# Seven block products for eight in the w_out matmul of an mLSTM-and-MLP kernel

## The chip, the cores and the metric

The kernel runs on one core of a Trainium2 chip. The metric is the device time of one execution in microseconds; smaller is better. Engines are named as in the profile: PE is TensorE (PEld its weight loads), DVE is VectorE, ACT is ScalarE, POOL is GpSimd, SP is SyncE.

## The reference

An mLSTM cell for batch 4, 8 heads, 768 steps and head dimension 40; its output (3072 tokens of 320 features) goes through an MLP with 2048 hidden features and the activation h - tanh(h). All is fp32, with weights that arrive as float64.

```python
for t in range(S):
    m_new = np.maximum(f_gate[:, :, t] + m, i_gate[:, :, t])
    f_stab = np.exp(f_gate[:, :, t] + m - m_new)
    i_stab = np.exp(i_gate[:, :, t] - m_new)
    m = m_new
    C = f_stab[:, :, None, None] * C + i_stab[:, :, None, None] * np.einsum('bhd,bhe->bhde', vt, kt)
    n = f_stab[:, :, None] * n + i_stab[:, :, None] * kt
    h_tilde = np.einsum('bhde,bhe->bhd', C, qt)
    denom = np.maximum(np.abs(np.einsum('bhd,bhd->bh', n, qt)[:, :, None]), 1.0)
    y[:, :, t] = h_tilde / (1.0 + np.exp(-o_gate[:, :, t])) / denom
x = y.transpose(0, 2, 1, 3).reshape(B * S, H * D)      # 3072 x 320
h = x @ w_in                                           # 320 x 2048
return (h - np.tanh(h)) @ w_out                        # 2048 x 320
```

## The kernel before

**Units.** The cell is cut into 24 units: 128 steps of one batch entry, all heads; unit n is chunk n // 4 of batch entry n % 4. A unit's steps are: `scores` (the products `ps`, masked on DVE into `P`), `inter` and `intra` (products of the state and of `P` with the scaled values `vs`, both into the PSUM tile `ph`), `gate` (on DVE: three short `den` rows, then `o` and `ys`, the last of which reads `ph` too), `update` (products `pc`, from which DVE's two `state` rows make the next chunk's state), and `turn` (three transposes into `px`, which ACT copies into `xT`).

**Groups, pairs, items.** Two units make a group of 256 tokens; there are 12 groups. The 16 blocks of 128 hidden features make 8 pairs. A (group, pair) takes an `up` (`ph_up` = xT times w_in: per feature block two full products of 256 columns and one over 64 rows, `w_rest`), a `shrink` (ACT: `z`, `q`; DVE: four `gt` rows, giving g = h - tanh h as a polynomial), and a `down`: four products `po` of 128x128 by 128x320, two token tiles times two feature blocks. Two pairs make an item; pairs 0, 1 and 8 stand alone. There are 50 items. The list of pairs first runs through the first four groups as the cell and the weights come (`RUNS`; partial sums go to `part`), then takes groups 4 to 11 one after another (`FIRST` = 4), each accumulated over its 8 pairs in `po` and copied out once.

**Order.** PE's order is written out: in step x of the main loop, `up` of item x, then `down` of item x - 1 (`LAG` = 1), and between them, in proportion to cost, the small steps of cell and weight conversion that `spread_over` put at x. A cell slot (`cell_slot`, line 510) holds the scores of unit s, the inside of unit o = s - 1 and the turn of x = s - 2. The order on DVE and ACT is the scheduler's from the main loop on (`Pinned.on = False`).

**Weights.** Each block of w_in and w_out is fetched as float64 bits by POOL and turned to fp32 by DVE and ACT (`weights`, rows `w_e`, `w_m`, `w_r`, then `w_in`, `w_rest`, `w_out`), eight staging buffers deep, in the first 150 us or so.

**PSUM.** Eight banks: `ph0`, `ph1` for `up`, `po0`, `po1` for `down` (line 580), two for scores, and two for the small tiles of the cell (`ph`, `pc`, `px` and those of the gates), a pool with `bufs=2` and one tag, line 173, from which each tile takes a free buffer:

```python
ps_b = ctx.enter_context(tc.tile_pool(name="ps_b", bufs=2, space=PSUM))
...
t["px"] = ps_b.tile([128, NK + 1, L], FP, name="px", tag="b")
```

Helpers record PE's, DVE's and ACT's operations, so the profile puts most of them on lines 102, 126 and 130, and tiles tell them apart.

Of the kernel before, what the change touches and what calls it, by code (L numbers as in the profile page):

```python
# [40 lines left out]
FP = mybir.dt.float32  # L44
# [28 lines left out]
def kernel(  # L73
# [96 lines left out]
    ps_h = ctx.enter_context(tc.tile_pool(name="ps_h", bufs=1, space=PSUM))  # L170
    ps_o = ctx.enter_context(tc.tile_pool(name="ps_o", bufs=1, space=PSUM))
    ps_a = ctx.enter_context(tc.tile_pool(name="ps_a", bufs=1, space=PSUM))
    ps_b = ctx.enter_context(tc.tile_pool(name="ps_b", bufs=2, space=PSUM))

# [97 lines left out]
    def gates(c0, c1, idle):  # L272

        t0, t1, cs, n = c0 * L, c1 * L, slice(c0, c1), c1 - c0
        at = slice(t0, t1)
        V.tensor_tensor_scan(out=m_sb[:, at], data0=f_sb[:, at], data1=i_sb[:, at],
                             initial=m_sb[:, t0 - 1:t0] if t0 else -1.0e30, op0=OP.add, op1=OP.max)
        if t0 == 0:

            V.memset(lf[:, 0:1], 0.0)  # L280
            t0 = 1
        V.tensor_tensor(out=lf[:, t0:t1], in0=f_sb[:, t0:t1], in1=m_sb[:, t0 - 1:t1 - 1], op=OP.add)
        V.tensor_tensor(out=lf[:, t0:t1], in0=lf[:, t0:t1], in1=m_sb[:, t0:t1], op=OP.subtract)
        V.tensor_tensor(out=i_sb[:, at], in0=i_sb[:, at], in1=m_sb[:, at], op=OP.subtract)

        cols = []
        for row in (lf, i_sb):
            p = ps_b.tile([L, NT, BH], FP, name="pcol", tag="b")
            for c in range(c0, c1):
                T.transpose(p[:, c, :], row[:, c * L:(c + 1) * L], ident[0:BH, 0:BH])  # L290
            cols.append(p[:, cs])
        V.tensor_copy(out=lfT[:, cs], in_=cols[0])
        A.activation(out=ei[:, 2, cs], in_=cols[1], func=AF.Exp)
        awake(idle)

        def sums_of(w):
            p = ps_b.tile([w.shape[1], NT, BH], FP, name="psum_lf", tag="b")
# [162 lines left out]
    def inter(n, j):  # L460
        t = un[n]
        if "ph" not in t:
            t["ph"] = ps_b.tile([L, H, D1], FP, name="ph", tag="b")
# [21 lines left out]
    def update(n, j):  # L485
        t = un[n]
        st = state[t["b"]][(t["c"] + 1) % 2]
        if j == 0:
            t["pc"] = ps_b.tile([TOP, HH, 2, D1], FP, name="pc", tag="b")
        T.matmul(t["pc"][:, j].rearrange("p two d -> p (two d)"), pair(t["k"], j), pair(t["vs"][:, 1], j), start=True, stop=True)  # L490
        if j < HH - 1:
            return
        for i in range(2):
            new, pc = st[:, :, i, :], t["pc"][:, :, i, :]
            if t["c"]:
                V.scalar_tensor_tensor(out=new, in0=pc, scalar=own[0:TOP, i:i + 1], in1=new, op0=OP.mult, op1=OP.add)
            else:
                V.tensor_single_scalar(new, pc, own[0:TOP, i:i + 1], op=OP.mult)

    def turn(n, j):  # L500
        t = un[n]
        if j == 0:
            t["px"] = ps_b.tile([128, NK + 1, L], FP, name="px", tag="b")
        T.transpose(t["px"][:, j, :], t["y"][:, FROM[j]:FROM[j] + 128], ident)
        if j == NK:
            g, tt = divmod(n, GT)
            A.copy(out=xT[g % NX][:, :, tt * L:(tt + 1) * L], in_=t["px"])
            un.pop(n)

    def cell_slot(s, o, x):  # L510


        steps = []
        if o is not None:
            prepare(o)
        if s is not None and s - 1 in un:
            prepare(s - 1)
        if s is not None:
            if s + 1 < NU and s + 1 not in ld:
                load_unit(s + 1)  # L520
            begin(s)
        for d in range(HH):
# [7 lines left out]
        if x is not None:  # L530
            steps += [(0.11, lambda j=j: turn(x, j)) for j in range(NK + 1)]
        return steps


    gT, po = {}, {}

    def up(some, shrink):

# [18 lines left out]
    def shrink(x):  # L557
        def steps(some, ph):
# [9 lines left out]
                V.scalar_tensor_tensor(out=gt[i], in0=ph[i], scalar=TINY_POLY[0], in1=z[i], op0=OP.mult, op1=OP.mult)  # L568
            for i in range(2):
                V.scalar_tensor_tensor(out=gt[i], in0=q[i], scalar=TINY_POLY[2], in1=gt[i], op0=OP.add, op1=OP.mult)  # L570

        return steps

    def down(x, some, g, p, first, last):
# [9 lines left out]
        def evict(tt):  # L584
            n = g * GT + tt
            if last < NP - 1:
                if first:
                    V.tensor_tensor(out=part[n], in0=po[tt], in1=part[n], op=OP.add)
                else:
                    A.copy(out=part[n], in_=po[tt])  # L590
                return
            ob = mlp.tile([128, DM], FP, name="ob", tag="ob")
# [4 lines left out]
            c, b = divmod(n, B)  # L597
            r0 = (b * NT + c) * L
            nc.scalar.dma_start(out=out[r0:r0 + L, :], in_=ob)

        return [(0.54, lambda i=i, tt=tt: product(i, tt)) for tt in range(GT) for i in range(2)]

# [12 lines left out]

    slots = [tuple(n if 0 <= n < NU else None for n in (s, s - 1, s - 2)) for s in range(NU + 2)]
    AHEAD = 3
    slots[AHEAD] = (3, 2, None)  # L620
    NS = len(slots)
# [5 lines left out]
    for g in range(FIRST, NG):  # L627
        pairs += [(g, p, 0, NP - 1) for p in range(NP)]

    ALONE = (0, 1, 8)  # L630
    items = []
    while sum(map(len, items)) < len(pairs):
        x = sum(map(len, items))
# [2 lines left out]
    def item(x):  # L636

        return min(i for i in range(len(items)) if sum(map(len, items[:i + 1])) > x)
# [19 lines left out]
    for i, (x0, x1) in enumerate(spans):  # L658
        begins[int(x0)].append((slots[AHEAD + i], x0, x1))

    first, steps = convert()
# [3 lines left out]
        due[p] = max(min(due[p], due[p + 1] - 1.25), 0.5)  # L667
    for p in range(1, NP):
        spread_over(steps[ready[p - 1]:ready[p]], due[p - 1], due[p])

    for fetch, _, _ in first:
        fetch()
# [52 lines left out]
    for x in range(len(items) + LAG):  # L725
# [2 lines left out]
        dense = []  # L728
        new = []
        for slot, x0, x1 in begins[x]:  # L730
            spread_over(cell_slot(*slot), x0, x1)
            if slot[0] is not None:
                new.append(slot[0])
        if x < len(items):
# [3 lines left out]
        dense += [(0.9, lambda n=n: halves(scores(n))) for n in new[1 if x < len(items) else 0:]]  # L738
        if x >= LAG:
            some = tuple(run[:2] for run in items[x - LAG])  # L740
            for i, run in enumerate(items[x - LAG]):
                dense += down(i, some, *run)
        merge(dense, [(cost, step) for _, cost, step in sorted(work[x], key=lambda w: w[0])])


# [4 lines left out]
    def rows_of_f():  # L750
# [11 lines left out]
        V.scalar_tensor_tensor(out=f, in0=f, scalar=1.0, in1=n, op0=OP.add, op1=OP.mult)  # L762


        row = ps_b.tile([NR, 2, L], FP, name="row", tag="b")
# [59 lines left out]
    with tc.If(nc.values_load(again, min_val=0, max_val=128,  # L825
                              skip_runtime_bounds_check_because="it counts partitions") > 0):
        T.last = V.last = A.last = None
        G.tensor_copy(out=diag, in_=ident.unsqueeze(1).to_broadcast([128, H, L]))
        V.tensor_copy(out=ei[:, 0], in_=ei[:, 2])
        V.memset(inv, 1.0)  # L830
        rows_of_f()
        for g in range(NG):
# [25 lines left out]
                            T.matmul(ob[tt], gts[i][:, p - p0, tt * L:(tt + 1) * L], w_out[:, 2 * p + i, :],  # L858
                                     start=(p == 0 and i == 0), stop=(p == NP - 1 and i == 1))
            for tt in range(GT):  # L860
                o = mlp.tile([128, DM], FP, name="ob", tag="ob")
# [44 lines left out]
```

## Time and profile before

| | |
|---|---|
| runs, us | 619.99, 620.53, 626.17 (median 620.53) |
| profiled execution, its own time, us | 618.87 |
| its span, first to last instruction, us | 617.2 |
| mean granted TensorE clock | 0.977 |
| PE busy, us | 573.7 (93%) |
| PEld busy, us | 444.0 (72%) |
| DVE busy, us | 297.4 (48%) |
| ACT busy, us | 194.7 (32%) |
| `po` products | 768 passes, 248.8 us |
| `ph_up` products, w_in and w_rest | 768 and 384 passes, 204.0 and 55.0 us |

An fp32 product is two passes on PE, so 384 `po` products are 768 rows. Busy time counts overlapping passes once, and a row's mean includes the tail that overlaps the next; the pitch of passes is read from their starts. In the rows of 40 slices a digit is tenths of a slice of 15.4 us.

### The profile page before, as it was taken

Reading aid. Unit: us, or ns where it says so; the run is one execution under the profiler, and the core shown is the slowest. Engines: PE = TensorE matmul, PEld = TensorE weight load, DVE = VectorE, ACT = ScalarE, POOL = GpSimd, SP = SyncE. Lnnn points to the kernel's source line nnn. Section 1 sums busy time; section 2 is a strip of 40 time slices with the busy share of each in tenths; the row PEclk is TensorE's granted clock in tenths of the full one; section 3 lists DMA queues with packets and bytes.
Section 4 is the critical chain, followed back from the end, with each engine's and each line's share of the span. In section 5 each row is a group of like instructions: output and inputs, shape, how many; then the busy total and the mean of one; then the engine's idle time right before and its main releaser. Section 6 shows DMA issues by size and latency. Waiting matters only on the chain.

```text
span 617.2 us, 8489 instructions
## 1 busy us (share of the span) xinstructions
PE 573.7 (93%) x3137; PEld 444.0 (72%) x3137; DVE 297.4 (48%) x716; ACT 194.7 (32%) x490; POOL 28.5 (5%) x60
## 2 busy tenths in 40 slices
PE   4965899998999999899999999999999999999995
PEld 1855777777787776777777787777778777767773
DVE  1679799999627334552623425325152333232231
ACT  1345554456123123221313214123141322232231
POOL 2022111220000000000000000000000000000000
PEclk9976699999999999999999999999999999999999
DMA  7665354452102010131212212011000000000000
GB/s 196 210 203 154 98 158 135 142 166 60 44 21 65 15 50 23 44 95 55 57 29 65 64 33 65 22 33 44 12 11 12 1 21 1 1 22 2 21 1 27
DMA packets 40865, 38.19 MB, mean 62 GB/s; under 512 B 3856, under 2 KB 38352, under 8 KB 40816
## 3 DMA queue, kind: packets, MB, share of 16 engines
q1 hardware_dynamic: 33000, 22.82, 12.9%
q0 software_dynamic: 2800, 9.18, 5.1%
q10 hardware_dynamic: 5016, 5.57, 2.7%
q8 instruction: 27, 0.44, 0.3%
q14 instruction: 22, 0.18, 0.1%
HBM read 33.62 MB, written 3.93 MB: 61 GB/s over the span
## 4 chain that ended last, share of the span: by engine, by line
PE 52%; issue 6%; ACT 2%; DVE 1%; ACTq 0%; DVEq 0%
PE ph_up L126 24%; PE po L126 23%; PE ph L126 3%; PE ps L126 1%; ACT q L102 1%; ACT z L102 1%; PE px L130 1%; PE pc L126 1%; DVE P L102 0%; ACT ob L102 0%; DVE gt L102 0%; DVE ob L102 0%; DVE part L102 0%; ACTq L102 0%; DVEq L102 0%
## 5 line engine op out<-in xcount | busy, mean ns | idle before, releaser
L126 PE MATMUL po<-w_out,gt 128*128 128x320 f32 x768 | 248.8, 449 | 12.4 <-DVE part L102 8.8
L126 PE MATMUL ph_up<-xT,w_in 128*128 128x256 f32 x768 | 204.0, 394 | 3.5 <-ACT xT L102 3.5
L102 DVE SCALAR_TENSOR_TENSOR gt<-ph_up,z 128x512 f32<-128x512 f32 (+1 forms) x100 | 62.5, 664 | 239.3 <-ACT z L102 239.2
L126 PEld LDWEIGHTS po<-w_out,gt 128*128 128x128 f32 x768 | 130.7, 191 | 57.3 <-DVE part L102 11.9
L126 PEld LDWEIGHTS ph_up<-xT,w_in 128*128 128x128 f32 x768 | 136.6, 193 | 22.8 <-ACT xT L102 4.6
L102 ACT ACTIVATE z<-ph_up 128x512 f32<-128x512 f32 (+1 forms) x100 | 57.1, 576 | 265.8 <-issue 143.7
L126 PEld LDWEIGHTS ph<-vs,P 128*128 128x128 f32 x384 | 70.7, 205 | 24.9 <-issue 6.3
L126 PE MATMUL ph<-vs,P 128*128 128x41 f32 x384 | 64.0, 264 | 5.9 <-DVE vs L102 3.1
L102 ACT ACTIVATE q<-z,tiny 128x512 f32<-128x512 f32 (+1 forms) x100 | 64.7, 700 | 0.0
L102 DVE SCALAR_TENSOR_TENSOR gt<-q,gt 128x512 f32<-128x512 f32 (+1 forms) x100 | 62.3, 661 | 0.0
L126 PE MATMUL ph_up<-xT,w_rest 64*128 64x256 f32 x384 | 55.0, 403 | 0.0
L126 PEld LDWEIGHTS ph_up<-xT,w_rest 64*128 64x128 f32 x384 | 32.9, 186 | 15.5 <-issue 12.5
L126 PEld LDWEIGHTS ph<-state,q 80*128 80x128 f32 x160 | 29.8, 194 | 8.3 <-ACT xT L102 0.5
L102 DVE TENSOR_TENSOR P<-ps,upto 128x512 f32<-128x512 f32 x48 | 30.9, 681 | 2.3 <-PE ps L126 2.3
L126 PEld LDWEIGHTS pc<-vs,k 128*80 128x80 f32 x160 | 22.3, 162 | 11.2 <-issue 3.2
L126 PEld LDWEIGHTS ps<-qz,kz 40*128 40x128 f32 x384 | 28.0, 205 | 2.2 <-DVE P L102 0.8
L126 PE MATMUL ph<-state,q 80*128 80x82 f32 x160 | 29.0, 262 | 0.3
L126 PE MATMUL ps<-qz,kz 40*128 40x128 f32 x384 | 29.1, 293 | 0.0
L126 PE MATMUL pc<-vs,k 128*80 128x82 f32 x160 | 25.2, 255 | 1.2 <-issue 1.2
L102 ACT ACTIVATE w_e<-w_e,rebias 128x256 int32<-128x256 int32 (+2 forms) x40 | 19.9, 503 | 20.1 <-DVE w_e L102 19.9
L102 ACT ACTIVATE w_r<-w 128x256 f32<-128x256 uint32 (+2 forms) x40 | 17.3, 434 | 20.1 <-DVE w_in L102 9.8
L335 POOL DMA_DIRECT2D w<-in_moe_w_in x35 | 19.0, 547 | 47.4 <-issue 21.0
(75 smaller groups left out, 305.6 us busy)
## 6 DMA issues: line engine op xcount, KB each, us to landing
w<-in_moe_w_out POOLq DMA_DIRECT2D x14, 320.0 KB, 3.5
kz<-in_kT SPq DMA_DIRECT2D x48, 80.0 KB
v<-in_v SPq DMA_DIRECT2D x24, 160.0 KB
k<-in_k SPq DMA_DIRECT2D x24, 160.0 KB
o<-in_o_gate SPq DMA_DIRECT2D x24, 160.0 KB
out<-ob ACTq DMA_DIRECT2D x24, 160.0 KB
qz<-in_qT SPq DMA_DIRECT2D x44, 80.0 KB
q<-in_qT SPq DMA_DIRECT2D x40, 80.0 KB
```

The source lines that it names most:

```text
L102: i = method(*args, **kwargs)
L126: return cls.keep(nc.tensor.matmul(*args, **kwargs))
L130: return cls.keep(nc.tensor.transpose(*args, **kwargs))
L335: queue.dma_start(out=to[rows, cols], in_=part)
```

## The change

For groups 4 to 10 (`SEVEN`) the `down` of a pair is computed in the seven-product form: the two token tiles by two feature blocks of g, and the two feature blocks by two halves of 160 output columns of w_out, are taken as 2x2 blocks; seven block products of 128x128 by 128x160 take the place of eight (four products of 320 columns). For this DVE makes four sums of w_out's blocks per pair once (`sums_of_weights`, 128x160 each) and four sums of g per item (`sums_of_g`, 128x256 each). The seven results of a group are gathered in three PSUM banks, `pS0`, `pS1` and `pS2`, and `put_together` joins them at the group's end into the two output tiles.

The third bank, `pS2`, is b1, one of the cell's two. The small tiles now come from the helper `small`, which hands out the tags b0 and b1 in turn; from the first slot that ends after item 18 on, b1 is taken off its list. From there `cell_slot` runs in the form `single`: inside, gate, update and turn of one unit one after the other in the one bank, with empty steps (`pause`) between, and the turn in the same slot as the inside, so there is one slot less. Pair 31 becomes an item of its own, so that items 18 to 49 hold two pairs of one group each; the slots after item 7 span 2.47 items each instead of 2.25.

```diff
-    ps_b = ctx.enter_context(tc.tile_pool(name="ps_b", bufs=2, space=PSUM))
+    ps_b = ctx.enter_context(tc.tile_pool(name="ps_b", bufs=1, space=PSUM))
+    banks = ["b0", "b1"]
+    def small(shape, name):
+        banks.append(banks.pop(0))
+        return ps_b.tile(shape, FP, name=name, tag=banks[-1])
...
-            t["px"] = ps_b.tile([128, NK + 1, L], FP, name="px", tag="b")
+            t["px"] = small([128, NK + 1, L], "px")
...
+        if single:
+            steps += turning
+            if o is not None:
+                for d in range(HH):
+                    steps.append((0.22 if o >= B else 0.0, lambda d=d: inter(o, d)))
+                    steps += [(0.22, lambda h=h: intra(o, h)) for h in (2 * d, 2 * d + 1)]
+                steps.append((0.0, lambda: gate(o)))
+                un[o]["turned"] = True
+                pause = [(0.0, lambda: None)]
+                steps += 5 * pause
+                if o + B < NU:
+                    steps += [(0.18, lambda j=j: update(o, j)) for j in range(HH)] + 4 * pause
+                steps += [(0.11, lambda j=j: turn(o, j)) for j in range(NK + 1)] + 4 * pause
+            return steps
...
+    def sums_of_weights(p):
+        t = wT[p] = conv.tile([128, 4, HM], FP, name="wT", tag="w64", bufs=8)
+        even, odd = (w_out[:, 2 * p + i, :].rearrange("p (two n) -> p two n", two=2) for i in range(2))
+        return [... for o, a, b in (
+            (t[:, 0], even[:, 1], even[:, 0]), (t[:, 1], odd[:, 1], t[:, 0]),
+            (t[:, 2], odd[:, 1], even[:, 1]), (t[:, 3], odd[:, 0], t[:, 1]))]
+    def sums_of_g(some):
...
+        V.tensor_tensor(out=s3, in0=a[0][0], in1=a[1][0], op=OP.subtract)
+        V.tensor_tensor(out=s1, in0=a[1][0], in1=a[1][1], op=OP.add)
+        V.tensor_tensor(out=s2, in0=s1, in1=a[0][0], op=OP.subtract)
+        V.tensor_tensor(out=s4, in0=a[0][1], in1=s2, op=OP.subtract)
+    def down_seven(some):
...
+        for k in range(7):
+            for x, (_, p) in enumerate(some):
...
+                where, a, b = (
+                    ((0, 2), a11, even[:, 0]), ((0, 0), a12, odd[:, 0]), ((2, 1), a22, wT[p][:, 3]),
+                    ((1, 1), s3, wT[p][:, 2]), ((1, 0), s1, wT[p][:, 0]), ((0, 1), s2, wT[p][:, 1]),
+                    ((2, 0), s4, odd[:, 1]))[k]
+                steps.append((0.27, lambda where=where, a=a, x=x, b=b: product(where, a, x, b)))
+        if last:
+            steps.append((0.0, lambda: put_together(g)))
+    def put_together(g):
...
+        A.copy(out=a, in_=bank[0][:, 2])
+        V.tensor_tensor(out=ob[:, 0:5:4], in0=bank[0][:, 0:2], in1=twice(a), op=OP.add)
+        V.tensor_tensor(out=u, in0=bank[1], in1=twice(ob[:, 4]), op=OP.add)
+        V.tensor_tensor(out=ob[:, 3], in0=bank[1][:, 0], in1=u[:, 1], op=OP.add)
+        V.tensor_tensor(out=ob[:, 1:3], in0=bank[2], in1=u, op=OP.add)
+        for tt in range(GT):
+            send(g * GT + tt, ob[:, 2 * tt:2 * tt + 2].rearrange("p two n -> p (two n)"))
...
+            if some[0][0] in SEVEN:
+                sums_of_g(some)
...
-    ALONE = (0, 1, 8)
+    ALONE = (0, 1, 8, FIRST * NP - 1)
...
+    for p in range(NP):
+        seven_at = seven - 1 + p / 2
+        spread_over([(0.0, lambda p=p: [step() for _, step in sums_of_weights(p)])], seven_at, seven_at + 0.5)
...
-            spread_over(cell_slot(*slot), x0, x1)
+            if x1 > seven - 1 and len(banks) > 1:
+                banks.remove("b1")
+            spread_over(cell_slot(*slot, single=len(banks) == 1), x0, x1)
```

More of the change, by code (lines that the diff above doesn't have):

```diff
@@ L287, in gates @@
         for row in (lf, i_sb):
-            p = ps_b.tile([L, NT, BH], FP, name="pcol", tag="b")
+            p = small([L, NT, BH], "pcol")
             for c in range(c0, c1):
@@ L296, in sums_of @@
         def sums_of(w):
-            p = ps_b.tile([w.shape[1], NT, BH], FP, name="psum_lf", tag="b")
+            p = small([w.shape[1], NT, BH], "psum_lf")
             T.matmul(p[:, cs].rearrange("p c n -> p (c n)"), w, lfT[:, cs].rearrange("p c n -> p (c n)"),
@@ L462, in inter @@
         if "ph" not in t:
-            t["ph"] = ps_b.tile([L, H, D1], FP, name="ph", tag="b")
+            t["ph"] = small([L, H, D1], "ph")
         if t["c"]:
@@ L488, in update @@
         if j == 0:
-            t["pc"] = ps_b.tile([TOP, HH, 2, D1], FP, name="pc", tag="b")
+            t["pc"] = small([TOP, HH, 2, D1], "pc")
         T.matmul(t["pc"][:, j].rearrange("p two d -> p (two d)"), pair(t["k"], j), pair(t["vs"][:, 1], j), start=True, stop=True)
@@ L507, in turn, with cell_slot @@
             A.copy(out=xT[g % NX][:, :, tt * L:(tt + 1) * L], in_=t["px"])
-            un.pop(n)
-    def cell_slot(s, o, x):
+    def cell_slot(s, o, x, single=False):
         steps = []
@@ L521, in cell_slot @@
             begin(s)
+        if x is not None and "turned" not in un[x]:
+            turning = [(0.11, lambda j=j: turn(x, j)) for j in range(NK + 1)]
+        else:
+            turning = []
+        if single:
[12 more added lines that the diff above has]
+            return steps
         for d in range(HH):
@@ L529, in cell_slot @@
             steps.append((0.0, lambda: gate(o)))
-        if x is not None:
-            steps += [(0.11, lambda j=j: turn(x, j)) for j in range(NK + 1)]
-        return steps
-    gT, po = {}, {}
+        return steps + turning
+    gT, po = {}, {}
+    HM = DM // 2
+    SEVEN = range(FIRST, NG - 1)
+    gS, wT, pS = {}, {}, {}
+    def sums_of_weights(p):
+        t = wT[p] = conv.tile([128, 4, HM], FP, name="wT", tag="w64", bufs=8)
+        even, odd = (w_out[:, 2 * p + i, :].rearrange("p (two n) -> p two n", two=2) for i in range(2))
+        sub = OP.subtract
+        return [(1.0, lambda o=o, a=a, b=b: V.tensor_tensor(out=o, in0=a, in1=b, op=sub)) for o, a, b in (
+            (t[:, 0], even[:, 1], even[:, 0]), (t[:, 1], odd[:, 1], t[:, 0]),
+            (t[:, 2], odd[:, 1], even[:, 1]), (t[:, 3], odd[:, 0], t[:, 1]))]
@@ new lines, in sums_of_g @@
+    def sums_of_g(some):
+        a = [[gT[some][i][:, :, tt * L:(tt + 1) * L] for i in range(2)] for tt in range(GT)]
+        s1, s2, s3 = (conv.tile([128, 2, L], FP, name=name, tag=tag, bufs=3)[:, 0:len(some)]
+                      for name, tag in (("s1", "w_e"), ("s2", "w_m"), ("s3", "w_r")))
+        s4 = mlp.tile([128, 2, L], FP, name="s4", tag="s4")[:, 0:len(some)]
+        gS[some] = s1, s2, s3, s4
+        V.tensor_tensor(out=s3, in0=a[0][0], in1=a[1][0], op=OP.subtract)
+        V.tensor_tensor(out=s1, in0=a[1][0], in1=a[1][1], op=OP.add)
+        V.tensor_tensor(out=s2, in0=s1, in1=a[0][0], op=OP.subtract)
+        V.tensor_tensor(out=s4, in0=a[0][1], in1=s2, op=OP.subtract)
@@ new lines, in down_seven, with product @@
+    def down_seven(some):
+        g = some[0][0]
+        first, last = some[0][1] == 0, some[-1][1] == NP - 1
+        def product(where, a, x, b):
+            bank, block = where
+            if g not in pS:
+                pS[g] = [ps_o.tile([128, 3, HM], FP, name="pS0", tag="po0"),
+                         ps_o.tile([128, 2, HM], FP, name="pS1", tag="po1"),
+                         ps_b.tile([128, 2, HM], FP, name="pS2", tag="b1")]
+                started[:] = [False] * 3
+            T.matmul(pS[g][bank][:, block], a, b, start=not started[bank], stop=last and x == len(some) - 1,
+                     skip_group_check=True)
+            started[bank] = True
+        steps = []
+        for k in range(7):
+            for x, (_, p) in enumerate(some):
+                even, odd = (w_out[:, 2 * p + i, :].rearrange("p (two n) -> p two n", two=2) for i in range(2))
+                a11, a12, a21, a22 = (gT[some][i][:, x, tt * L:(tt + 1) * L] for tt in range(GT) for i in range(2))
+                s1, s2, s3, s4 = (t[:, x] for t in gS[some])
+                where, a, b = (
[5 more added lines that the diff above has]
+            steps.append((0.0, lambda: put_together(g)))
+        return steps
@@ new lines, with twice @@
+    started = [False] * 3
+    def put_together(g):
+        bank = pS[g]
+        ob = mlp.tile([128, 5, HM], FP, name="ob", tag="ob")
+        a = mlp.tile([128, HM], FP, name="a", tag="a", bufs=1)
+        u = conv.tile([128, 2, HM], FP, name="u", tag="w_m", bufs=3)
+        def twice(t):
+            return t.unsqueeze(1).to_broadcast([128, 2, HM])
+        A.copy(out=a, in_=bank[0][:, 2])
[5 more added lines that the diff above has]
+            send(g * GT + tt, ob[:, 2 * tt:2 * tt + 2].rearrange("p two n -> p (two n)"))
@@ L537, in up, with send @@
+    def send(n, ob):
+        c, b = divmod(n, B)
+        r0 = (b * NT + c) * L
+        nc.scalar.dma_start(out=out[r0:r0 + L, :], in_=ob)
     def up(some, shrink):
@@ L591, in evict @@
                 return
-            ob = mlp.tile([128, DM], FP, name="ob", tag="ob")
+            ob = mlp.tile([128, 5, HM], FP, name="ob", tag="ob")[:, 0:2].rearrange("p two n -> p (two n)")
             if first:
@@ L596, in evict @@
                 A.copy(out=ob, in_=po[tt])
-            c, b = divmod(n, B)
-            r0 = (b * NT + c) * L
-            nc.scalar.dma_start(out=out[r0:r0 + L, :], in_=ob)
+            send(n, ob)
         return [(0.54, lambda i=i, tt=tt: product(i, tt)) for tt in range(GT) for i in range(2)]
@@ L614, in merge @@
             step()
-    slots = [tuple(n if 0 <= n < NU else None for n in (s, s - 1, s - 2)) for s in range(NU + 2)]
+    slots = [tuple(n if 0 <= n < NU else None for n in (s, s - 1, s - 2)) for s in range(NU + 1)]
     AHEAD = 3
@@ L659 @@
         begins[int(x0)].append((slots[AHEAD + i], x0, x1))
+    seven = item(FIRST * NP) + LAG
     first, steps = convert()
@@ L740 @@
             some = tuple(run[:2] for run in items[x - LAG])
-            for i, run in enumerate(items[x - LAG]):
-                dense += down(i, some, *run)
+            if some[0][0] in SEVEN:
+                dense += down_seven(some)
+            else:
+                for i, run in enumerate(items[x - LAG]):
+                    dense += down(i, some, *run)
         merge(dense, [(cost, step) for _, cost, step in sorted(work[x], key=lambda w: w[0])])
@@ L762, in rows_of_f @@
         V.scalar_tensor_tensor(out=f, in0=f, scalar=1.0, in1=n, op0=OP.add, op1=OP.mult)
-        row = ps_b.tile([NR, 2, L], FP, name="row", tag="b")
+        row = small([NR, 2, L], "row")
         for i in range(2):
@@ L827 @@
         T.last = V.last = A.last = None
+        banks[:] = ["b0", "b1"]
         G.tensor_copy(out=diag, in_=ident.unsqueeze(1).to_broadcast([128, H, L]))
@@ L860 @@
             for tt in range(GT):
-                o = mlp.tile([128, DM], FP, name="ob", tag="ob")
+                o = mlp.tile([128, 5, HM], FP, name="ob", tag="ob")[:, 0:2].rearrange("p two n -> p (two n)")
                 A.copy(out=o, in_=ob[tt])
```

## Prediction

> **What bounds the kernel now.** I read first the busy rows and the slices of the page, then the windows, the chain of waits, the groups, and last the timeline at single stages.
>
> ```profile
> PE 573.7 (93%) x3137; PEld 444.0 (72%) x3137; DVE 297.4 (48%) x716; ACT 194.7 (32%) x490; POOL 28.5 (5%) x60
> PE   4965899998999999899999999999999999999995
> DVE  1679799999627334552623425325152333232231
> PEclk9976699999999999999999999999999999999999
> PE 52%; issue 6%; ACT 2%; DVE 1%; ACTq 0%; DVEq 0%
> L126 PE MATMUL po<-w_out,gt 128*128 128x320 f32 x768 | 248.8, 449 | 12.4 <-DVE part L102 8.8
> ```
>
> TensorE is nearly always busy and is most of the chain that ended last. But DVE stands at nine tenths in slices four to nine, some 60 to 150 us, while weights are converted. The windows give the stages:
>
> ```profile
> 92.00:122.00 30.00, 27.26 (x176) 22.14 (x177) 28.10 (x81) 14.87 (x36) 6.63 (x12) 1.00 0.46 138
> 122.00:154.00 32.00, 30.29 (x190) 24.37 (x189) 30.82 (x92) 19.15 (x48) 4.44 (x8) 1.00 0.40 113
> 287.00:440.00 153.00, 152.87 (x863) 119.99 (x862) 57.74 (x117) 43.10 (x108) 0.00 (x0) 1.00 0.14 42
> ```
>
> The columns are the stretch and its length, then busy us (instructions) of PE, PEld, DVE, ACT and POOL, the granted clock, DMA share and GB/s. From 92 to 154 us DVE works 58.9 of 62 us; from 287 to 440 us PE idles 0.13 of 153 us, so there a matmul saved is time saved and a wait added is time lost.
>
> **The products (saves 14.1 us).** The pitch of a matmul is read from merged rows of the timeline (start, length, engine, count): every fp32 product is two passes.
>
> ```profile
> 573.62 3.62 PE L126 MATMUL ph_up<-xT,w_in 128*128 128x256 f32 x16
> 570.66 3.12 PE L126 MATMUL po<-w_out,gt 128*128 128x320 f32 x11
> 398.17 0.30 PEld L126 LDWEIGHTS po<-w_out,gt 128*128 128x128 f32 x2
> ```
>
> Without the last pass's own length (0.38 and 0.43 us), 15 pitches take 3.24 us, so 0.216 us for 256 columns, and 10 take 2.69, so 0.269 for 320: 0.83 ns a column, and 0.136 us for 160. Removed are 7 groups x 8 pairs x 4 products = 224, or 448 passes x 0.269 = 120.6 us; added are 56 x 7 = 392, or 784 x 0.136 = 106.5 us. That is -14.1 us if each new weight load hides. The third line has two loads (0.19 us each) in 0.30 us: the second starts 0.11 us after the first, less than 0.136. If instead a load held the array for its whole 0.191 us, it would be 784 x 0.191 = 149.7 us, +29.1; I take the pitch, since loads at 0.11 us are seen. The page "TensorE: Matmul & The Clock Gate", section "Back-to-back issue gap", of the Trainium skill speaks against a linear scaling: in a stream of loads and matmuls it gives about 81 ns at 128 columns, where the matmul alone would take about 56. As an estimate by that page, 25 ns on each of 784 passes would be 19.6 us and turn -14.1 into +5.5.
>
> **Items start with groups (saves 2.1 us).** Pair 31 now stands alone, so a group ends with an item. Before, it ended inside one, and the next product waited for the copy out of its bank:
>
> ```profile
> 581.24 2.15 PE L126 MATMUL po<-w_out,gt 128*128 128x320 f32 x7 [0.58 <-ACT ob L102]
> ```
>
> Between first `ph_up` passes an undisturbed late item takes 9.02 us, the two with such a boundary (573.62 to 583.50 and 536.57 to 546.56 with one transpose of 0.11) 9.88 and 9.99: 0.85 more each, and an item at 496.5 has 0.4 more. Now a whole `up` of 4.6 us lies between; without that cover the new evictions (three DVE operations of 0.48, one of 0.33, an ACT copy of about 0.30) would cost 2.1 us for each of 7 groups. The last item grows from one pair to two: the last `gt` row ends 3.4 us after an `up`, under 4.3 us of products of the item before, so nothing; uncovered, 3.4 us.
>
> **New work on DVE (no time of its own).** Sums of g: 28 items x 4 x 0.415 us (the row 128x256 `w_in<-w_r,w_e`) = 46.5 us; sums of weights 32 x 0.33 = 10.4; evictions 7 x 1.8 = 12.4. Together 69 us in some 300, where DVE is busy 38% (57.7 of 153 above). An item's sums end 3.4 + 1.7 = 5.0 us after its `up`; their products follow a `down` and an `up` later, 3.9 + 4.6 = 8.5 us. Cover gone, 1 to 2 us an item, 28 to 56 us. What these 69 us do reach is the cell's queue, next.
>
> **The cell in one bank (costs 25 us).** From item 16.9 to 44 `ph`, `pc` and `px` share one bank, so PE's first write of each waits for the last reader of the one before, and everything behind it waits too, the dense products first: PE's queue is in order. Before, two banks hid this. I counted the PE rows that stand between, in the order in which the changed kernel's instructions stand on each engine, at the pitches above (small products 0.22 us), for units 13 to 23:
> - `ph` to the next tile: 0.65, 1.62, 1.47, 1.52, 1.47, 1.95, 1.74, then without update 2.39, 1.74, 2.54, 1.74 us. The gate chain (`den` three times, `o`, `ys`), from the last `ph` product to the end of `ys`, takes 2.24 us with a short queue (four units from 355 to 425 us). Late by 1.59, 0.62, 0.77, 0.72, 0.77, 0.29, 0.50, 0, 0.50, 0, 0.50: 6.3 us.
> - In six gates one or two sums (taken as 0.83 us) now stand between the gate's own rows, in two also the eviction (1.8 us): 5.0 + 3.6 = 8.6.
> - `pc` to `px`: 1.26 to 1.98 us between, while `state` ends 0.95 us after the last `pc` product: free. But in units 15, 17 and 19 the second `state` row stands behind the next item's four `gt` rows and two sums: 3.36 + 0.76 + 0.38 = 4.5 us after that `up`, where `px` stands 1.65 after it: 3 x 2.85 = 8.5.
> - `px` to `ph`: 0.1 to 1.4 us between, the copy `xT` ends 0.79 after the last transpose, in a few rows 2.3: 2.0.
>
> The sum is 25.4 us. From below, with every reader at its shortest (1.96, 0.95, 0.79), 4.2. From above, every reader as late as the latest in the trace (5.6, 3.5 and 2.3 us): 11 x 5.6 - 18.8, 7 x 3.5 - 11.0 and 11 x 2.3 - 11.8, together 70. I take 25, from rows of the same stage.
>
> **Two banks, but in strict turn (costs 22 us).** The helper `small` hands out b0 and b1 alternately, from the first instruction on. A slot makes `ph` of unit n, `pc` of n, `px` of n-1, so `px` now always gets the bank of `ph`, and the transposes, which stand just behind the last `ph` products, wait for the whole gate of the current unit. Before, they did not:
>
> ```profile
> 138.66 0.64 PE L126 MATMUL ph<-vs,P 128*128 128x41 f32 x4
> 139.75 0.49 PE L130 MATMUL px<-ident,ys 128*128 128x128 f32 x3
> 144.62 0.48 DVE L102 TENSOR_TENSOR ys<-ph,o 128x320 f32<-128x320 f32 x1
> ```
>
> `px` (of unit 7) starts at 139.75, while `ys` of unit 8 reads `ph` until 145.10: it sits in the other bank, that of `pc`, free by then. In strict turn it would start 5.3 us later. The same difference for units 3 to 12: 4.6, 2.0, 2.9, 2.5, 0.6, 5.3, 0.5, 0.9, 1.5, 3.8, together 24.7 us. Behind it on PE stand all products; DVE, 95% busy here, gains a little in each wait, so I take 22. Below: if DVE's order moved the gates forward, 0. Above: 24.7 and the three longest once more, since the changed order has conversion rows further ahead (63.5 us of them before `ys` of unit 7, 47.2 before): 38.
>
> In the window 36 to 67 us, with PE waits up to 2.8 us, the granted clock was 0.65:
>
> ```profile
> 36.00:67.00 31.00, 19.08 (x109) 16.20 (x110) 26.57 (x78) 13.65 (x36) 6.58 (x13) 0.65 0.51 152
> ```
>
> The same page, section "The HAM clock gate", has the clock fall to half after an idle window of about 3.4 us; an estimate by it is half a window, 1.7 us, for each of three waits that long, 5 us more.
>
> **The sum.** 618.87 (span 617.2 and 1.67 around it) - 14.1 - 2.1 + 25.4 + 22 = 650.1 us; the median of the runs, 620.53, lies 1.66 above the profiled run: 652.
>
> **The rivals.**
> - *Faster: the bank waits are short.* One mechanism, in the one-bank stage and ahead of it: readers come at once, because `gate` is reached earlier on DVE than its place says. Then 4.2 and 0: 618.87 - 16.2 + 4.2 + 1.66 = 608.5. For it: 62% idle DVE from 287 us on. Against: PE has under 2 us between the tiles in nine of eleven gates, the chain takes 1.96 at best. It decides when both waits together fall under 16.2 us. Chance 0.05; the waits just cancelling, no change, 0.03.
> - *Only one of the two waits is real.* With the one-bank wait alone 618.87 - 16.2 + 25.4 + 1.66 = 630; with the other alone 626. For it: the pool might have been alternating before; against: the three lines above. Chance 0.20.
> - *The stalls pull the clock down.* A row in which PE worked at half clock is 36 to 67 us (0.65); if 92 to 154 us, with 57.6 us of PE work, fell to a clock of 0.85, 10 us come on top: 662. Chance 0.07.
> - *A weight load holds the array.* +29.1 for -14.1: 695. Against it loads 0.11 us apart. Chance 0.03.
> - That the change doesn't do what it says: the order has 392 products of 160 columns and 160 of 320, so no.
>
> **How the numbers follow.** The forecast (both waits, 638 to 662) has 0.62, and its time is the prediction, 652. The range reaches down to the case of one wait (630) and up over the clock (668). A difference of 1% is about what a measurement of this kernel can tell from none: faster by more 0.05, within 0.03, slower by more 0.92.
>
> **What would show it.** Right: `pS` passes 0.136 us apart; PE idle ahead of `px` with DVE `ys` as releaser in the first 260 us; idle ahead of `pc`, `px` and `ph` from about 300 to 570 us; some 47 us of such idle. Wrong: PE gapless from 300 us on, or `pS` passes at 0.19 us, or a span under 627.

## The result and the profile after

The changed kernel is slower, and by more than the range allowed for.

| | before | after |
|---|---|---|
| runs, us, median (lowest to highest) | 620.46 (619.99 to 626.17) | 678.67 (676.09 to 679.79) |
| ratio to before, 95% interval | | 1.0909 [1.0839, 1.098] |
| span, us | 617.2 | 677.4 |
| mean granted clock | 0.977 | 0.914 |
| PE busy, us | 573.7 | 590.0 |
| PE idle (span less busy), us | 43.5 | 87.4 |
| PE at half clock from 36 us on, us | 29.0 | 96.7 |
| PE busy in it, us | 20.1 | 79.4 |

The last two rows are summed over the windows in which the clock reads one half; in the finest windows it reads 1 or one half. They start at 36 us because the clock of the kernel before is not to be trusted ahead of that:

```profile
10.00:28.00 18.00, 12.73 (x67) 10.25 (x68) 7.32 (x20) 6.04 (x15) 0.57 (x1) 1.00 0.74 219
23.17 0.63 PE L126 MATMUL awake<-diag 128*128 128x512 bf16 x1
29.11 0.39 PE L126 MATMUL awake<-diag 128*128 128x512 bf16 x1
10.00:28.00 18.00, 12.60 (x63) 10.03 (x65) 6.58 (x18) 6.14 (x15) 0.57 (x1) 0.52 0.72 215
24.14 0.63 PE L131 MATMUL awake<-diag 128*128 128x512 bf16 x1
```

The first three lines are of the kernel before, the last two of the changed one. The same `awake` matmul takes 0.63 us in both at 23 and 24 us, and 0.39 us later; but the clock reads 1.00 in the one and 0.52 in the other. So the mean of 0.977 leaves out some 20 us at half clock at the start of that trace (most other runs of the same kernel read 0.95 to 0.96), and the changed kernel's 0.914 has to be compared with some 0.96.

The table holds most of the answer: 43.9 us more idle, where the prediction's waits and spared waits come to 25.4 + 22 - 2.1 = 45.3; but busy time rose by 16.3 us, where the products were to take 14.1 away. What is missing, 30.4 us, goes with 67.7 us more at half clock, in which PE is busy for 59.3 us more; if that work takes twice its time, half of it is lost, 29.7 us.

The page of the changed kernel, first its busy rows and slices, then two of its groups:

```profile
PE 590.0 (87%) x3471; PEld 488.9 (72%) x3473; DVE 355.3 (52%) x888; ACT 191.7 (28%) x483; POOL 28.8 (4%) x60
PE   4974977787989798988998899899989999989996
DVE  1679878989342623363646346444526345534421
PEclk8575676899899989999999799989989899989999
L131 PE MATMUL po<-w_out,gt 128*128 128x320 f32 x320 | 110.5, 469 | 9.5 <-DVE part L107 9.4
L135 PE MATMUL px<-ident,ys 128*128 128x128 f32 x72 | 20.6, 323 | 43.5 <-DVE ys L107 34.6
```

The PE row has four sevens and an eight in slices six to ten (some 85 to 170 us), where before it had four nines and an eight. The clock row is lower in slices six to eight too, and here and there later. The transposes `px`, 20.6 us of work, have 43.5 us of idle time in front of them. The waits of PE, each with the us in total, the count and the longest:

```profile
PE px L135 <- DVE ys L107: 34.6, 12, 5.2
PE po L131 <- DVE part L107: 9.4, 8, 1.7
PE px L135 <- DVE state L107: 8.8, 5, 2.7
...
PE pc L131 <- DVE ys L107: 5.6, 5, 2.2
PE ph L131 <- DVE ys L107: 3.7, 1, 3.7
```

Before, `px` waited 1.3 us for `den` and 0.8 for `state` and had no wait for `ys` in the list. The first, third and fourth lines are waits that the prediction named. The fifth is one wait at 56 us, again for a `ys`, which it did not name. The two stages and some short stretches of the second, in the columns of the windows (the clock is the first of the last three numbers):

```profile
36.00:160.00 124.00, 96.07 (x529) 79.53 (x528) 105.81 (x317) 56.41 (x146) 22.85 (x42) 0.77 0.41 124
160.00:303.00 143.00, 123.17 (x647) 93.52 (x645) 61.79 (x138) 34.19 (x85) 0.00 (x0) 0.94 0.12 34
303.00:614.00 311.00, 287.62 (x1867) 251.59 (x1868) 150.78 (x342) 77.78 (x195) 0.00 (x0) 0.97 0.11 33
318.00:323.00 5.00, 4.17 (x25) 3.61 (x27) 0.87 (x3) 0.69 (x2) 0.00 (x0) 1.00 0.22 73
382.00:387.00 5.00, 3.94 (x19) 3.93 (x20) 2.73 (x7) 0.22 (x1) 0.00 (x0) 0.66 0.10 34
387.00:440.00 53.00, 50.22 (x346) 43.77 (x344) 26.11 (x58) 14.61 (x37) 0.00 (x0) 1.00 0.16 47
440.00:445.00 5.00, 3.56 (x17) 3.56 (x18) 2.36 (x7) 0.02 (x1) 0.00 (x0) 0.66 0.11 33
445.00:498.00 53.00, 50.40 (x347) 44.52 (x345) 25.54 (x58) 14.90 (x37) 0.00 (x0) 1.00 0.11 32
498.00:503.00 5.00, 3.46 (x17) 3.45 (x18) 2.47 (x7) 0.00 (x0) 0.00 (x0) 0.66 0.02 3
```

From 36 to 160 us the clock is 0.77, where the same stretch of before has 0.89; PE executes 529 matmuls there against 660. From 303 us on, PE idles 23.4 of 311 us; before, it idled 0.85 of the 251 us from 303 to 554. The short rows show what the prediction's sum had left out: the clock falls in those 5 us in which a long wait ends (a mean of 0.66, which is 3.4 us at one half and the rest at one), and is 1.00 in the 53 us between. In the first of them, 318 to 323 us, a wait of 1.61 us ahead of `pc` ends, and its clock stays at 1.00.

### The profile page after: what moved, and what is told of

Its sections match the earlier page's. It is cut to its first block, busy times and chain, and to the rows that moved or that the text cites. A ratio compares the mean times of both kernels' runs of the same rounds, so it can differ in the third digit from the quotient of the medians.

```text
span 677.4 us, 9300 instructions
## 1 busy us (share of the span) xinstructions
PE 590.0 (87%) x3471; PEld 488.9 (72%) x3473; DVE 355.3 (52%) x888; ACT 191.7 (28%) x483; POOL 28.8 (4%) x60
## 5 line engine op out<-in xcount | busy, mean ns | idle before, releaser
L131 PE MATMUL ph_up<-xT,w_in 128*128 128x256 f32 x768 | 217.5, 412 | 3.2 <-ACT xT L107 3.2
L131 PEld LDWEIGHTS ph_up<-xT,w_in 128*128 128x128 f32 x768 | 142.0, 203 | 18.8 <-ACT xT L107 4.3
L131 PE MATMUL po<-w_out,gt 128*128 128x320 f32 x320 | 110.5, 469 | 9.5 <-DVE part L107 9.4
L131 PEld LDWEIGHTS po<-w_out,gt 128*128 128x128 f32 x320 | 56.9, 201 | 29.7 <-DVE part L107 12.1
L131 PE MATMUL pS<-wT,s 128*128 128x160 f32 x336 | 60.5, 318 | 0.0
L135 PE MATMUL px<-ident,ys 128*128 128x128 f32 x72 | 20.6, 323 | 43.5 <-DVE ys L107 34.6
L131 PEld LDWEIGHTS pS<-wT,s 128*128 128x128 f32 x336 | 51.8, 203 | 0.1
L135 PEld LDWEIGHTS px<-ident,ys 128*128 128x128 f32 x72 | 10.9, 161 | 51.4 <-issue 48.3
L131 PEld LDWEIGHTS ph_up<-xT,w_rest 64*128 64x128 f32 x384 | 33.1, 187 | 14.7 <-issue 11.8
L131 PE MATMUL pS<-w_out,gt 128*128 128x160 f32 x224 | 39.8, 313 | 0.0
L131 PEld LDWEIGHTS pS<-w_out,gt 128*128 128x128 f32 x224 | 31.6, 190 | 4.0 <-issue 3.6
```

What stands on the lines that cost most here:

```text
L131: return cls.keep(nc.tensor.matmul(*args, **kwargs))
L135: return cls.keep(nc.tensor.transpose(*args, **kwargs))
```

## The experiments

The theory: the two PSUM waits cost what they were forecast to in idle time, and the matmuls that follow each of the longer ones run at half clock, which costs some 30 us more. The rivals: the idle time is that of the new DVE work, not of the banks; or the 30 us belong to the seven products, whose weight loads do not hide. Ratios are to the kernel before, run on the same chip (medians 619.48 and 619.47 us). The last two columns are those of the table above, from 36 us on (before: 29.0 and 20.1); the mean clock of e9_eight lacks its first 28 us like that of the kernel before.

| label | median, us | ratio, 95% | span | clock | PE busy | PE idle | half clock | PE busy in it |
|---|---|---|---|---|---|---|---|---|
| e1_turn | 669.39 | 1.0812 [1.0774, 1.0851] | 668.7 | 0.931 | 592.3 | 76.4 | 72.2 | 56.5 |
| e2_pool | 632.9 | 1.0218 [1.0196, 1.0239] | 633.4 | 0.942 | 573.3 | 60.1 | 47.8 | 39.5 |
| e5_spaced | 601.9 | 0.9727 [0.9701, 0.9753] | 600.1 | 0.954 | 558.0 | 42.1 | 34.9 | 23.3 |
| e9_eight | 616.6 | 0.998 [0.9939, 1.0021] | 613.2 | 0.977 | 571.4 | 41.8 | 28.3 | 20.1 |
| e6_stir | 661.91 | 1.0663 [1.0595, 1.0731] | 660.9 | 0.952 | 608.1 | 52.8 | 42.8 | 34.0 |
| e8_alone | 614.26 | 0.9904 [0.9872, 0.9937] | 612.9 | 0.953 | 573.8 | 39.1 | 36.8 | 27.1 |

### e1_turn: the kernel before, with the strict turn alone

```diff
-    ps_b = ctx.enter_context(tc.tile_pool(name="ps_b", bufs=2, space=PSUM))
+    ps_b = ctx.enter_context(tc.tile_pool(name="ps_b", bufs=1, space=PSUM))
+    banks = ["b0", "b1"]
+    def small(shape, name):
+        banks.append(banks.pop(0))
+        return ps_b.tile(shape, FP, name=name, tag=banks[-1])
...
-            t["px"] = ps_b.tile([128, NK + 1, L], FP, name="px", tag="b")
+            t["px"] = small([128, NK + 1, L], "px")
```

(and so for the other small tiles)

> The kernel before, with one edit: the cell's small tiles come from two tags handed out strictly in turn, so the transposes get the bank of ph. Everything else as before, po products too. Theory A (the strict turn makes the transposes wait for the current unit's gate, and the waits let the granted clock fall): PE idle ahead of px with ys as releaser, some 22 us in units 3 to 12 as in the changed kernel (22.8 there) and about 14 more in units 13 to 22 (the same differences read from the trace of before: 1.6, 1.4, 1.1, 3.0, 1.0, 1.1, 0.3, 2.8, 1.9, 0.3), and half-clock time well over the 31 us of before; in all 660 to 685 us. Rival B (the early loss comes from the seven-product form and its DVE rows, not from the banks): no change, 617 to 625 us.

Measured: 669.39 us, 49.9 more than before, with not one product, sum or group changed. Two rows of the page, and the first of PE's waits:

```profile
PE 592.3 (89%) x3137; PEld 456.2 (68%) x3137; DVE 298.6 (45%) x716; ACT 194.4 (29%) x490; POOL 28.7 (4%) x60
PEclk7676676899899999989999999999999999999998
```

```profile
PE px L130 <- DVE ys L102: 36.4, 17, 5.2
```

The idle time rises by 76.4 - 43.5 = 32.9 us. Busy time rises by 592.3 - 573.7 = 18.6 with the same 3137 matmuls: there the same work simply took longer, with 36.4 us more of it at half clock, half of which is 18.2. Ahead of `px` of units 2 to 11 the waits are 5.2, 2.7, 4.0, 3.4, 0.7, 4.2, 0.5, 0.9, 1.5 and 3.8 us, 27.0 in all; the prediction's list, from the trace of before, has 4.6, 2.0, 2.9, 2.5, 0.6, 5.3, 0.5, 0.9, 1.5 and 3.8. Later ones add 9.4 us, where some 14 were expected. So a part of the change that leaves the arithmetic alone makes most of the loss, and more than a third of that is no wait at all.

### e2_pool: the changed kernel, with a free choice of buffer

```diff
-    ps_b = ctx.enter_context(tc.tile_pool(name="ps_b", bufs=1, space=PSUM))
+    ps_b = ctx.enter_context(tc.tile_pool(name="ps_b", bufs=2, space=PSUM))
...
-        banks.append(banks.pop(0))
-        return ps_b.tile(shape, FP, name=name, tag=banks[-1])
+        return ps_b.tile(shape, FP, name=name, tag="b")
...
-                          ps_b.tile([128, 2, HM], FP, name="pS2", tag="b1")]
+                          ps_b.tile([128, 2, HM], FP, name="pS2", tag="b")]
```

While `pS2` lives, the cell still has one buffer.

> The changed kernel, with one edit: the small tiles and pS2 come from one tag with two buffers again, so a tile takes whichever bank is free; the one-bank stage stays, as pS2 holds the other buffer. Theory A: the px waits of the first 300 us go (23 us of idle) and the half-clock windows there with them (about 20 us of work), the 22 us of waits after 300 us stay with their clock windows: 630 to 645 us. Rival B (the early loss is DVE's order, drawn forward by the new rows): the first 300 us stay as they are in the changed kernel, 670 to 680 us.

Measured: 632.9 us, 45.8 less than the changed kernel. From 36 to 160 us the clock is back at 0.88. What is left of the waits:

```profile
PE px L135 <- DVE state L107: 9.6, 7, 2.7
PE px L135 <- DVE ys L107: 6.7, 3, 3.3
```

The wait for `ys` falls from 34.6 to 6.7 us. Before 300 us `px` has 2.1 us of waits left (0.8 for `state`, 1.3 for `den`), as before the change; the rest lies in the one-bank stage, 19.1 us with those of `pc`. So the early idle time belongs to the turn and not to DVE's new work, which is all still here.

### e5_spaced: e2_pool, with room between the steps of the one-bank stage

```diff
-                pause = [(0.0, lambda: None)]
+                pause = [(0.6, lambda: None)]
```

The empty steps now have a weight, so that `spread_over` puts dense products in their places, between `gate` and `update`, `update` and `turn`, and after the turn.

> The kernel of the free choice of banks, with one further edit: the empty steps between gate, update and turn in the one-bank stage get a weight of 0.6 in the merge (0.0 before), so that dense products lie between the tiles. Theory A: the one-bank waits go too, no half-clock window after 300 us, and what is left of the change is its passes and the aligned items: 620.5 - 14.1 - 2.1, so 600 to 608 us. Rival C (the seven-product form itself is dear: weight loads, or sums that come late): pS passes over 0.14 us apart or PE idle ahead of pS, 620 us or more.

Measured: 601.9 us, 31.0 less than e2_pool, and 17.6 less than the kernel before: this version beats both kernels. The first line is its window from 303 to 554 us, and the second e2_pool's 5 us around one wait for `state`:

```profile
303.00:554.00 251.00, 251.00 (x1718) 226.29 (x1717) 138.25 (x307) 71.36 (x177) 0.00 (x0) 1.00 0.10 29
```

```profile
396.00:401.00 5.00, 4.68 (x22) 4.63 (x23) 1.24 (x4) 0.48 (x1) 0.00 (x0) 0.66 0.11 33
```

With one bank and the seven products, PE is busy for 251.00 of 251 us at full clock, beside 138 us of work on DVE. So the bank waits were a matter of the distance between steps in PE's order, and DVE's 57.9 us of new work cost nothing there. Between the profiled spans lie 33.3 us. Of these 18.0 are idle time; from 29 us on (e2_pool's first stretch lasts to 38 us) PE works 22.9 us less at half clock (24.0 against 46.9), worth half of that, 11.5; about 4 us I cannot put to an item.

### e9_eight: e5_spaced, with the eight products

```diff
-    SEVEN = range(FIRST, NG - 1)
+    SEVEN = range(0)
...
-        spread_over([(0.0, lambda p=p: [step() for _, step in sums_of_weights(p)])], seven_at, seven_at + 0.5)
+        spread_over([(0.0, lambda p=p: None)], seven_at, seven_at + 0.5)
```

All groups run as groups 0 to 3 and 11 do, without sums and without `pS0` to `pS2`, so that the cell keeps both buffers; its order stays.

> The spaced kernel with the eight products of before in all groups (po of 320 columns; no sums of weights or of g). Theory A: 616 to 620 us, some 14 us above the spaced kernel, the difference being 448 passes of 0.269 us against 784 of 0.136. Rival C: at or below the spaced kernel.

Measured: 616.6 us, so that the seven products are worth 601.9 - 616.6 = -14.7 us in medians (-13.4 in busy time). One late item of e5_spaced, with the first row of the next, shows the pitch:

```profile
545.17 3.62 PE L131 MATMUL ph_up<-xT,w_in 128*128 128x256 f32 x16
548.72 1.14 PE L131 MATMUL ph_up<-xT,w_rest 64*128 64x256 f32 x8
549.78 1.35 PE L131 MATMUL pS<-w_out,gt 128*128 128x160 f32 x8
550.98 0.71 PE L131 MATMUL pS<-wT,gt 128*128 128x160 f32 x4
551.52 1.79 PE L131 MATMUL pS<-wT,s 128*128 128x160 f32 x12
553.15 0.71 PE L131 MATMUL pS<-w_out,s 128*128 128x160 f32 x4
553.69 3.62 PE L131 MATMUL ph_up<-xT,w_in 128*128 128x256 f32 x16
```

Twelve passes from 551.52 to 553.15 are 0.136 us each. The item from 545.17 to 553.69 takes 8.52 us, where an undisturbed one of before takes 9.02: 0.50 less, as 16 x 0.269 - 28 x 0.136 = 0.50 has it for the 28 passes of these rows in place of 16. The weight loads hide; the rival that they hold the array (0.19 us a pass) is out. The kernel has its other runs up to 622.76 us, so the difference is good to a few us only; the pitch is the firmer evidence.

### e6_stir: the changed kernel, with idle matmuls in the places of the waits

```diff
+    def stir(what, n):
+        count = STIR.get((what, n), 0)
+        if count:
+            full = ps_a.tile([128, 512], FP, name="stir", tag="a1")
+            row = diag.rearrange("p h t -> p (h t)")
+            for _ in range(count):
+                T.matmul(full, row[:, 0:128], row[:, 0:512], start=True, stop=True)
...
-            turning = [(0.11, lambda j=j: turn(x, j)) for j in range(NK + 1)]
+            turning = [(0.0, lambda: stir("px", x))] + [(0.11, lambda j=j: turn(x, j)) for j in range(NK + 1)]
```

`STIR` gives 18 awaited tiles (`px` of units 2 to 5 and 7 to 10, and `px`, `pc` in the one-bank stage) 3 to 22 matmuls each, 193 in all, whose result nothing reads. All waits, sums and products of the changed kernel stay.

> The changed kernel as it is, with idle matmuls (bf16, 512 columns, into a score bank that is free) put ahead of 18 of the tiles that PE waited for: 193 of them, each count made a little shorter than the wait in the changed kernel's trace, 41.6 us in all at 0.216 us each. They do no work of the computation and take no wait away. Theory A (what the prediction lacked is the granted clock, which falls in the waits): half-clock time drops from 119 us to under 60, and the time falls by 15 to 28 us, to 650 to 664 us, though more is issued. Rival D (the lack lies elsewhere, in DVE or in longer waits than forecast): no gain, 677 us or more.

Measured: 661.91 us, 16.8 less than the changed kernel, though it issues 193 additional matmuls, 41.7 us at 0.216 us each.

```profile
PE 608.1 (92%) x3646; PEld 488.9 (74%) x3666; DVE 355.6 (54%) x888; ACT 192.0 (29%) x483; POOL 28.4 (4%) x60
PEclk8575799999999899999799999999999999999999
```

Its busy time without the filler is 608.1 - 41.7 = 566.4 us, 23.6 less than the 590.0 of the changed kernel for the same work. The filler took 34.6 us out of the idle time and lengthened the stretches by the other 7.1: -23.6 + 7.1 = -16.5, the difference of the spans. That is the clock by itself: at least 23.6 of the 30.4 us that were missing come back when PE has something to do in the waits (two lots of filler ran in part at half clock themselves and took some 3 us more than is priced here, so the other work saved that much more). Over the whole span 63 us at half clock remain, where under 60 were expected. Most lie before 160 us (the clock is 0.88 from 36 to 160 us, 1.00 from 365 to 600); a wait of 3.7 us ahead of `ph` is one that the filler does not cover, and one lot of filler itself waits 3.6 us for the `P` that reads its bank, with a fall of the clock behind it.

### e8_alone: the kernel before, with pair 31 as an item of its own

```diff
-    ALONE = (0, 1, 8)
+    ALONE = (0, 1, 8, FIRST * NP - 1)
```

> The kernel before, with one edit: pair 31 is an item of its own, so that groups end with items; the slots of the cell after item 7 span a little more. Theory: the two waits of 0.58 us for the copy out of po at 544 and 581 us go, 1.5 to 3 us less, 617 to 619 us. Rival: the moved slots cost as much, no change.

Measured: 614.26 us, 5.2 less than before, and under the 617 to 619 that were expected. Two waits of before go that I had not seen, for DVE's `ob`:

```profile
272.33 0.81 PE L126 MATMUL po<-w_out,gt 128*128 128x320 f32 x2 [0.96 <-DVE ob L102]
285.23 0.81 PE L126 MATMUL po<-w_out,gt 128*128 128x320 f32 x2 [1.04 <-DVE ob L102]
```

Idle time falls by 43.5 - 39.1 = 4.4 us, of which these two make 2.0. The two waits of 0.58 us make another 1.2. The clock reads lower than before (0.953 against 0.977), but most of that is the start that is missing in the trace of before: from 36 us on it is 36.8 us at half clock against 29.0, all but the end of it before 75 us, and PE busy time is the same (573.8).

## Why the prediction was right in direction and short in size

From the kernel before to the changed one the experiments make a path of single steps, in medians: aligned items (e8_alone) -5.2, the cell's new order (e9_eight) +2.3 (within the spread of its runs), seven products (e5_spaced) -14.7, no room between the steps in one bank (e2_pool) +31.0, the strict turn +45.8. They give the terms of the sum with their clock:

| term | forecast, us | idle time, us | with its clock, us |
|---|---|---|---|
| seven products | -14.1 | | -14.7 |
| items start with groups | -2.1 | -4.4 | -5.2 |
| cell in one bank | +25.4 | +22.7 (counted), +18.0 (e2_pool to e5_spaced) | +31.0 |
| strict turn | +22 | +25.8 (counted), +27.3 (to e2_pool), +32.9 (e1_turn) | +45.8 (49.9 in e1_turn) |

In e1_turn the turn lasts to the end of the kernel, in the changed one to 300 us. The idle time of all came out near the forecast (43.9 for 45.3) in part by luck: the turn was priced some 4 us too low, the bank and the items some 5 us too high.

- **The products: right.** The pitch of 0.136 us is there, and the loads hide. The Trainium skill's page "TensorE: Matmul & The Clock Gate", section "Back-to-back issue gap", led to an estimate of 19.6 us for loads in such a stream, which would have made this term a loss of 5.5; the runs show -14.7, and the measurement decides.
- **New work on DVE: right.** It costs nothing in e5_spaced. What it cost in the changed kernel was what the prediction had under the one bank, above all the second `state` row behind `gt` rows and sums. The timeline of the changed kernel at one of the three places:

```profile
378.99 0.39 DVE L107 SCALAR_TENSOR_TENSOR state<-pc,own,state 80x164 f32<-80x164 f32 x1 [7.00 <-PE pc L131]
...
380.67 1.28 DVE L107 SCALAR_TENSOR_TENSOR gt<-q,gt 128x512 f32<-128x512 f32 x2
381.87 0.75 DVE L107 TENSOR_TENSOR s<-gt 128x256 f32<-128x256 f32 x2
382.54 0.38 DVE L107 SCALAR_TENSOR_TENSOR state<-pc,own,state 80x164 f32<-80x164 f32 x1
...
383.06 0.45 PE L135 MATMUL px<-ident,ys 128*128 128x128 f32 x1 [2.71 <-DVE state L107]
```

Here the first `state` row runs at 378.99, the second only at 382.54, after four `gt` rows (two are left out here) and two sums, and `px` waits 2.71 us. Three such waits of 2.85 us were forecast; three of 2.71 came (ending at 383.1, 441.4 and 499.5 us).

- **The one bank: right in idle time.** 25.4 us were forecast, and 22.7 us of waits ahead of `px`, `pc` and `ph` are counted after 303 us: 8.8 for `state` (8.5 forecast), 13.0 behind the gate (14.9) and 0.9 for the copy `xT` (2.0).
- **The strict turn: right in mechanism, some 4 us short in idle time.** The ten transposes that wait for the gates of units 3 to 12 (`px` of units 2 to 11) wait 27.9 us in the changed kernel, 25.8 more than the 2.1 that they waited before, against 22 in the sum (24.7 before the discount for DVE). The wait of 3.7 us ahead of `ph` at 56 us is of the turn too (5.1 in e1_turn); before, that place had one of 2.8. The transposes of unit 7 in the timeline, which wait for `ys` of unit 8 as the prediction had it (5.3 us there, 4.41 here):

```profile
168.05 0.48 DVE L107 TENSOR_TENSOR ys<-ph,o 128x320 f32<-128x320 f32 x1
168.68 0.88 PE L135 MATMUL px<-ident,ys 128*128 128x128 f32 x3 [4.41 <-DVE ys L107]
```

- **Aligned items: undersized by 3.1 us.** I priced the boundaries of groups 4 and later and took two of them as typical, and overlooked the two waits for DVE's `ob` at 272 and 285 us, which stand in the list of waits of the kernel before.
- **The clock: the step that failed.** It stood in the prediction as a sentence with 5 us and as a rival with 10 us at a chance of 0.07, and in the sum not at all. It was 30.4 us (busy time up by 16.3 where 14.1 were to go), and at least 23.6 of them were taken back by idle matmuls alone. With it the prediction's 652 becomes 682, within 4 us of the result. The place that the rival named did come near what it said, a clock of 0.86 from 92 to 154 us (0.85 there), but that holds only 16 us of PE work at half clock of the 59.3. What I did wrong was to price the clock by the three longest waits. The section "The HAM clock gate" of the named page sets the condition at an idle window of about 3.4 us, and I counted waits of that length. In the runs here waits from 1.94 us on are followed by a fall, and there were some 20 more stretches of 3.4 us than before (67.7 / 3.4), not three. The trace of before could have told: it had the clock at 0.65 from 36 to 67 us, where no PE wait was longer than 2.8 us. I showed that row and then set it aside for the page's figure. The same page, section "A second HAM failure mode: psum-queue depth-cycling", says that short idle times of PE between groups of matmuls that go through PSUM banks in turn were seen to make the clock swing; it gives no length for them. The runs here fit that, with waits of some 2 us and more.

## What to carry to other kernels

A wait of some 2 us or more ahead of TensorE costs twice: price its length, and then half of the work that PE does at half clock behind it (here 30 us on top of 44), and read from the trace of before how short a wait already brings the clock down. Read the first stretch of the clock against a matmul of known length, since a trace can lack it. When PSUM gets tight, look at which reader each bank waits for before looking at the arithmetic: giving tiles out in strict turn instead of from whichever buffer is free cost 45.8 us, and a few products set between the steps that share a bank were worth 31.0. With both mended the seven-product form takes 601.9 us, 0.9727 [0.9701, 0.9753] of the kernel before.

## What the runs showed of the hardware

- From 300 us on, where the stretches are easy to tell apart, the changed kernel has six PE waits of 2.23 to 3.30 us (ending at 372, 383, 441, 499, 527 and 604 us), and near the end of each begins one stretch of about 3.4 us at half clock; after those of 1.70 us and less there is none. The rows of 318 to 323 and of 382 to 387 us above show one of each. Earlier, a wait of 1.94 us was the shortest that was followed by one.
- It hangs on when the wait falls. In all eight traces the changes of the clock lie a whole number of steps of 3.413 us apart. Cut along these steps, the changed kernel has:

```profile
198.46:201.88 3.42, 1.49 (x9) 0.96 (x8) 2.15 (x6) 0.22 (x1) 0.00 (x0) 1.00 0.18 46
201.88:205.29 3.41, 3.41 (x10) 2.70 (x9) 0.00 (x0) 0.47 (x1) 0.00 (x0) 0.50 0.17 50
300.87:304.28 3.41, 1.71 (x8) 1.02 (x7) 2.83 (x6) 0.84 (x2) 0.00 (x0) 1.00 0.34 103
304.28:307.70 3.42, 2.48 (x12) 1.58 (x11) 0.98 (x2) 0.48 (x1) 0.00 (x0) 1.00 0.24 85
```

  After a step in which PE was busy for 1.49 us (0.44 of it) the next is at half clock; after one with 1.71 us (0.50) it is not. From 75 us on the eight traces have 27 steps at full clock in which PE was busy for 0.44 of the step or less, and all 27 are followed by one at half clock; of the 1234 in which it was busy for 0.50 or more none is. Earlier, two steps with 0.64 and 0.77 were followed by one too, which this does not explain.
- Work at half clock cost half its time. In the changed kernel PE is busy at half clock for 59.3 us more than before, half of which is 29.7, and 30.4 were missing; in e1_turn it is 36.4 us more, half of which is 18.2, and busy time rose by 18.6. So it is the work in such a stretch that has to be counted, not the stretch: of the 29.0 us of before PE is busy for 20.1.
